# Attention and feed-forward on one core: the order of the first loads, the first k turned by blocks, and a split last tile

## The chip, the cores and the metric

The kernel runs on one core of one Trainium2 chip. The metric is the device time of one execution in microseconds (us); lower is better. The median of 6 runs before the change is 440.61 us (439.31 to 441.51).

## What is computed

Grouped-query attention, followed by a feed-forward layer with a squared relu. There are 8 batches, 16 query heads on 4 key/value heads (four query heads share one), 384 positions and 64 elements a head. The feed-forward takes the 3072 rows of attention output (8 x 384) through 1024 -> 2048 -> 1024.

```python
k = np.repeat(k, 4, axis=1); v = np.repeat(v, 4, axis=1)
scores = q @ k.transpose(0, 1, 3, 2) / sqrt(64)
attn = exp(scores - max(scores)); attn = attn / (sum(attn) + 1e-9)
x = (attn @ v).transpose(0, 2, 1, 3).reshape(3072, 1024)
out = maximum(x @ w_in, 0) ** 2 @ w_out
```

Inputs and output are float32; the kernel computes in bfloat16 with float32 accumulation.

## The kernel before

**A recorder.** The program is written as one list of operations (`R.add`, line 23). Each names its engine, what it reads and what it writes. From that list the recorder derives semaphores: an operation waits for the last writer of what it reads, and for writer and readers of what it overwrites; `after` adds further waits. Each engine runs its own operations in the order of the list, so a wait holds up all that stands behind it on that engine. DMAs are issued by an engine too: SP ("sync"), ACT ("scalar") or GpSimd ("gpsimd", POOL in the profile); an issue that waits holds up that engine's queue.

**Units.** The batches are called b0 to b7 here. A batch has 8 pairs of query heads (`NPB`), so there are 64 pairs; pair n of b0 uses k group n // 2. The 384 positions are three blocks of 128 (`NJ`). For a pair, scores are made transposed (keys on the partitions), exponentiated on ACT into `expT`, and multiplied with `v_aug` (v with a column of ones, so that the sum comes along) on PE into the bank `po`; DVE divides (`rinv`, `o_sb`, lines 416 and 419). Output tiles are transposed into `xT`, which the feed-forward reads: up-projection (line 437), relu on DVE (444), square on ACT (446), down-projection (455), copy to `y_sb` on DVE (464), store by SP (467).

**b0, the start.** b0's operands come as float32 by plain loads: k group 0 and then v and k groups 1 to 3 from SP (`first_k`, line 201; v, line 214), q in four pieces from ACT (`first_q`, line 207). Group 0 of k is cast and duplicated on DVE (`dup_k`, line 235), as is the first q piece (`cast_q`, line 230). All the others are cast on GpSimd. They are transposed on PE by a matmul against an identity and copied out of PSUM by DVE (`turn_on_pe`, lines 302 and 310; `first_kT`, `first_qT`). In the loop `for n in range(NPB)` the scores come block by block (`scores_unit`, 362 and 368), the turns of the next pair between them, and `attend(n - 1, ...)` in two halves. `idle(...)` are matmuls of zeros, with no use but to keep PE busy.

**GpSimd's order at the start** (lines 240 to 266): cast_q(1), cast of v, dup_k(1), load_q(1), cast_q(2), load_k(1), cast_q(3), load_w_in(0), cast_q(4), dup_k(2), load_w_in(1), and so on to cast_q(7), load_v(1), the remaining weight blocks, load_w_out(0 and 1), and then k, q and v of b2. The loads of this list convert float32 to bfloat16 on the way; they go through one software queue, in this order. `load_q(1)` is b1's q, 768 KB as bfloat16; `load_k(1)` is b1's k, 192 KB.

**b1 and later.** b1's k is duplicated by DVE in `dup_all_k(1)` (line 326), at the end of n = 3 in the list, and turned on PE between the pairs 4 to 7 of b0 and after them. From b2 on `prepare(b)` (line 330) duplicates k on DVE and lets SP issue transposing DMAs: one for k (line 333, it reads `k_dup`), two for q (line 340, they read `q_st`, where `load_q(b)` puts it). Each finished pair of b1 and later goes to `xT` by a transposing DMA on SP (`put_x`, line 424). SP's list around b1 is: put_x and stores of b0's output, `prepare(2)`, then again put_x of the pairs 12 to 15 and stores in turn.

**The feed-forward.** It is a generator of small steps; `fill` takes as many of them between the attention parts as a credit allows. Batch b's feed-forward starts when attention of batch b + 1 is under way. An up step for one chunk of 128 hidden columns takes the eight `xT` tiles in two groups of four. A down tile (128 rows x 512 columns) accumulates 16 matmuls in one of two banks `f_ps` (`down_step`, line 450). At the end only down tiles of b7 are left; the last one is followed by its copy and its store.

Of the kernel before, what the change touches and what calls it, by code (L numbers as in the profile page):

```python
# [106 lines left out]
def bass_gqa_attention__then__ffn_squared_relu_kernel(  # L107
# [11 lines left out]
    B, H, S, D = 8, 16, 384, 64  # L119
    HKV = 4  # L120
    NJ = S // 128
# [6 lines left out]
    NST, NKS, NEX, NXT, NHR, NY, NO = 3, 2, 3, 3, 3, 4, 4  # L128

    R = Recorder(nc)  # L130
# [7 lines left out]
    k_f = sb("k_f", [128, HKV, NJ, D], f32)  # L138
# [58 lines left out]
            moe_w_out[:, i * 512:(i + 1) * 512].rearrange("(c p) f -> p c f", p=128)),  # L197
            writes=[("w_out", i)], dma=f"wo{i}")

    def first_k(g0, g1):  # L200
        R.add("sync", lambda e: e.dma_start(
            k_f[:, g0:g1].rearrange("p g j d -> p g (j d)"),
            k[0, g0:g1].rearrange("g (p j) d -> p g (j d)", j=NJ)),
            writes=[("k_f", g) for g in range(g0, g1)], dma=f"kf{g0}")

    def first_q(c0, c1):
        R.add("scalar", lambda e: e.dma_start(
            q_f[:, 2 * c0:2 * c1, :], q[0, 2 * c0:2 * c1].rearrange("h (p j) d -> p h (j d)", j=NJ)),
            writes=[("q_f", c) for c in range(c0, c1)], dma=f"qf{c0}")

    first_k(0, 1)
    first_q(0, 1)
    first_q(1, 2)
    R.add("sync", lambda e: e.dma_start(
        v_f.ap().rearrange("p g j d -> p g (j d)"), v[0].rearrange("g (p j) d -> p g (j d)", j=NJ)),
        writes=["v_f"], dma="vf")
    first_q(2, 4)
    first_k(1, 4)
    first_q(4, 8)

    R.add("vector", lambda e: e.memset(warm[:], 0.0), writes=["warm"])  # L221
    R.add("gpsimd", lambda g: g.memset(ident[:], 0.0), writes=["ident"])
# [6 lines left out]
    def cast_q(c, eng="gpsimd"):  # L229
        R.add(eng, lambda g: g.tensor_copy(q_st[0][:, 2 * c:2 * c + 2, :], q_f[:, 2 * c:2 * c + 2, :]),  # L230
              reads=[("q_f", c)], writes=[("q_st", 0, c)])

    def dup_k(g, eng):
        src = k_f[:, g].unsqueeze(2).to_broadcast([128, NJ, 2, D])
        R.add(eng, lambda e: e.tensor_copy(k_dup[0][:, g * NJ:(g + 1) * NJ], src),
              reads=[("k_f", g)], writes=[("k_dup", 0, g)])

    dup_k(0, "vector")
    cast_q(0, "vector")
    cast_q(1)  # L240
    R.add("gpsimd", lambda g: g.tensor_copy(
        v_aug[0][:, :, 0:D], v_f.ap().rearrange("p g j d -> p (g j) d")),
        reads=["v_f"], writes=[("v_aug", 0)])
    dup_k(1, "gpsimd")
    load_q(1)
    cast_q(2)
    load_k(1)
    cast_q(3)
    load_w_in(0)
    cast_q(4)  # L250
# [43 lines left out]
            return f_ps[i - 5].ap().bitcast(bf16)[:, 0:S], ("f_ps", i - 5)  # L294
        return sc_bf[:, i, 0:S], ("sc", i)

    def turn_on_pe(src, src_keys, dst, dst_key, banks, eng="vector"):
        ps, key = turn_bank(banks)

        def tr(pe):  # L300
            for t in range(NJ):
                m = pe.matmul(ps[:, t * 128:(t + 1) * 128], src[:, t * 128:(t + 1) * 128], ident[:],  # L302
                              is_transpose=True)
            return m

        R.add("tensor", tr, reads=[*src_keys, "ident"], writes=[key])
        if eng == "scalar":
            R.add(eng, lambda e: e.copy(dst, ps), reads=[key], writes=[dst_key])
        else:
            R.add(eng, lambda e: e.tensor_copy(dst, ps), reads=[key], writes=[dst_key])  # L310

    def first_kT(g, b=0, banks=RING):
        turn_on_pe(k_dup[b][:, g * NJ:(g + 1) * NJ].rearrange("p a x d -> p (a x d)"), [("k_dup", b, g)],
                   kT[b][:, g], ("kT", b, g), banks)

    def first_qT(c, b=0, banks=RING):
        turn_on_pe(q_st[b][:, 2 * c:2 * c + 2, :].rearrange("p h e -> p (h e)"), [("q_st", b, c)],
                   qT[b][:, c], ("qT", b, c), banks)

    def first_oT(c, banks=RING, eng="vector"):  # L320
        turn_on_pe(o_sb[c % NO].ap().rearrange("p i s d -> p (i s d)"), [("o_sb", c % NO, x) for x in range(2)],
                   xT[0][:, c], ("xT", 0, c), banks, eng)

    def dup_all_k(b, eng="vector"):
        src = k_st[b % NKS].ap().rearrange("p g j d -> p (g j) d").unsqueeze(2)
        R.add(eng, lambda e: e.tensor_copy(  # L326
            k_dup[b % 2][:, :, :, :], src.to_broadcast([128, HKV * NJ, 2, D])),
            reads=[("k_st", b % NKS)], writes=[("k_dup", b % 2, g) for g in range(HKV)])

    def prepare(b):  # L330
        st = b % NST
        dup_all_k(b)
        R.add("sync", lambda e: e.dma_start_transpose(
            kT[b % 2].ap().rearrange("p g (j c) -> p (g j) c", j=NJ),
            k_dup[b % 2].ap().rearrange("p a x d -> p (a x d)")),
            reads=[("k_dup", b % 2, g) for g in range(HKV)],
            writes=[("kT", b % 2, g) for g in range(HKV)], dma=f"kt{b % 2}")
        for part in range(2):
            cs = range(4 * part, 4 * part + 4)
            R.add("sync", lambda e, cs=cs: e.dma_start_transpose(  # L340
                qT[b % 2][:, cs.start:cs.stop, :].rearrange("p h (t c) -> p (h t) c", t=NJ),
                q_st[st][:, 2 * cs.start:2 * cs.stop, :].rearrange("p h e -> p (h e)")),
                reads=[("q_st", st, c) for c in cs], writes=[("qT", b % 2, c) for c in cs],
                dma=f"qt{b % 2}_{part}")
# [5 lines left out]

    def operands(p):
        b, c = p // NPB, p % NPB
        return kT[b % 2][:, c // 2], qT[b % 2][:, c], [("kT", b % 2, c // 2), ("qT", b % 2, c)]

    def scores_unit(p, j):
        u = (p * NJ + j) % 2
        kt, qt, keys = operands(p)

        def sc(pe):
            for x in range(2):  # L360
                rows = slice(64 * x, 64 * x + 64)
                m = pe.matmul(sc_ps[:, 2 * u + x, 0:S], kt[rows, j * 128:(j + 1) * 128], qt[rows, :])  # L362
            return m

        R.add("tensor", sc, reads=keys, writes=[("sc", 2 * u), ("sc", 2 * u + 1)])
        src = sc_ps[:, 2 * u:2 * u + 2, 0:S].rearrange("p x (t c) -> p x t c", t=NJ)
        dst = expT[p % NEX][:, j, :].rearrange("p (t x c) -> p x t c", x=2, t=NJ)
        R.add("scalar", lambda e: e.activation(dst, src, AF.Exp, scale=0.125),  # L368
              reads=[("sc", 2 * u), ("sc", 2 * u + 1)], writes=[("expT", p % NEX, j)])

    def scores_pair(p):
        kt, qt, keys = operands(p)
        half = NJ * S

        def piece(pe, x, j, c0, c1):
# [54 lines left out]
    tiles = [0]  # L430
# [16 lines left out]
                  reads=[("hr", r)], writes=[("h2T", b % 2, c)])  # L447
        return (k1 - k0) * 165

    def down_step(b, i, jj, part, u):  # L450
        yb = (b * 2 * NJ + jj * NJ + i) % NY

        def mm(pe):
            for c in range(4 * part, 4 * part + 4):
                m = pe.matmul(f_ps[u][:, :], h2T[b % 2][:, c, i * 128:(i + 1) * 128],  # L455
                              w_out_sb[:, c, jj * 512:(jj + 1) * 512],
                              start=(c == 0), stop=(c == NFC - 1))
            return m

        R.add("tensor", mm, reads=[("w_out", jj)] +  # L460
              [("h2T", b % 2, c) for c in range(4 * part, 4 * part + 4)], writes=[("f_ps", u)])
        if part == 3:
            half = slice(jj * 512, (jj + 1) * 512)
            R.add("vector", lambda e: e.tensor_copy(y_sb[yb][:, :], f_ps[u][:, :]),  # L464
                  reads=[("f_ps", u)], writes=[("y", yb)])
            rows = out[b * S:(b + 1) * S, :].rearrange("(p j) f -> j p f", j=NJ)[i]
            R.add("sync", lambda e: e.dma_start(rows[:, half], y_sb[yb][:, :]),
                  reads=[("y", yb)], writes=[("out", b, i, jj)], dma=f"y{yb}")
        return 4 * 216

    def feed_forward(b):
        first = 0
        if b == 0:
            for c, k in [(c, k) for c in range(3) for k in (0, 2, 4)] + [(c, 6) for c in range(3)]:
                yield up_step(b, c, k, k + 2, c, c)
            first = 3
        for c in range(first, NFC):
            for k in range(0, NKC, 4):
                yield up_step(b, c, k, k + 4, tiles[0] % 2, tiles[0] % NHR)
            tiles[0] += 1  # L480
        for jj in range(2):
            for i in range(NJ):
                for part in range(4):
                    yield down_step(b, i, jj, part, tiles[0] % 2)
                tiles[0] += 1


    ready = [0]
# [21 lines left out]
    turns += [lambda banks=RING, c=c: first_qT(c, 1, banks) for c in range(NPB)]  # L510

    idle(13)
    first_kT(0, banks=(4,))
    idle(1)
    first_qT(0, banks=(6,))
    for n in range(NPB):
        ring = (4, 6) if n < 4 else RING
        scores_unit(n, 0)
        if n >= 4:
            turns.pop(0)()  # L520
        else:
            idle(2 if n == 0 else 1)
        if n >= 1:
            attend(n - 1, 0)
        scores_unit(n, 1)
# [48 lines left out]
        ready[0] = max(0, n // NPB - 1)  # L574
    while next(ffn, None):
        pass
    R.add("sync", lambda e: e.nop(), reads=[("out", b, i, jj) for b in range(B) for i in range(NJ) for jj in range(2)])
    R.emit()


# [26 lines left out]
```

The softmax here doesn't subtract the row's maximum and nothing guards it: scores larger than these inputs give would overflow.

## Time and profile before

| what | us |
|---|---|
| median of 6 runs | 440.61 (439.31 to 441.51) |
| the profiled execution, its time | 439.11 |
| its span from the first to the last instruction | 436.9 |
| PE busy in the span | 427.5 (98%) |
| ACT, DVE, GpSimd busy | 199.4, 164.7, 34.2 |

All numbers of the profile come from that one execution. A row of instructions has a start, a length, the engine, the line, the operation, output tile <- input tiles and how many. "SPq", "ACTq" and "POOLq" are the instructions by which an engine issues DMAs. A part in brackets tells the idle time before an instruction and who ended it. A row of a DMA issue has the size of one and the time from issue to landing.

The first 40 us as a table of who does what first:

| event | starts at, us |
|---|---|
| first k (group 0) duplicated on DVE, first q piece cast | 3.40, 3.95 |
| first scores, first exp | 5.50, 6.04 |
| cast_q(1), cast of v, dup_k(1) on GpSimd | 5.72, 6.16, 7.17 |
| load_q(1), cast_q(2), load_k(1), cast_q(3), load_w_in(0) on GpSimd | 7.63, 8.91, 9.36, 10.11, 10.55 |
| dup_all_k(1) on DVE | 17.00 |
| last exp of b0 ends | 28.51 |
| first up-projection of the feed-forward | 27.90 |

ACT's 24 exps of b0 take 0.81 each; ACT is idle 5.8 us before them in sum, 1.66 of it before the exp at 19.46.

At the end of the span the last down tile's matmuls run to 433.76, the copy from 433.78 to 434.47, the last store is issued at 434.50 and takes 2.0 from issue to landing.

### The profile page before, as it was taken

Reading aid. Unit: us, or ns where it says so; the run is one execution under the profiler, and the core shown is the slowest. Engines: PE = TensorE matmul, PEld = TensorE weight load, DVE = VectorE, ACT = ScalarE, POOL = GpSimd, SP = SyncE. Lnnn points to the kernel's source line nnn. Section 1 sums busy time; section 2 is a strip of 40 time slices with the busy share of each in tenths; the row PEclk is TensorE's granted clock in tenths of the full one; section 3 lists DMA queues with packets and bytes.
Section 4 is the critical chain, followed back from the end, with each engine's and each line's share of the span. In section 5 each row is a group of like instructions: output and inputs, shape, how many; then the busy total and the mean of one; then the engine's idle time right before and its main releaser. Section 6 shows DMA issues by size and latency. Waiting matters only on the chain.

```text
span 436.9 us, 8195 instructions
## 1 busy us (share of the span) xinstructions
PE 427.5 (98%) x3580; PEld 239.2 (55%) x3615; DVE 164.7 (38%) x354; ACT 199.4 (46%) x210; POOL 34.2 (8%) x50
## 2 busy tenths in 40 slices
PE   8899999999999999999999999999999999999997
PEld 4565655556545654466545665556654565546543
DVE  2665433244323442244423443334522443324311
ACT  4766743466334563256523654336643366103300
POOL 5930000020000100020000200011000000000000
PEclk9999999999999999999999999999999999999999
DMA  7999999366722945238621856229542200220011
GB/s 223 192 197 203 193 206 195 125 79 68 167 66 68 121 86 105 89 61 102 128 92 59 111 76 135 69 81 127 70 109 75 67 11 18 68 83 24 2 72 72
DMA packets 95939, 44.70 MB, mean 102 GB/s; under 512 B 74400, under 2 KB 89760, under 8 KB 95904
## 3 DMA queue, kind: packets, MB, share of 16 engines
q0 software_dynamic: 34288, 16.65, 30.6%
q1 hardware_dynamic: 59504, 25.96, 25.4%
q10 hardware_dynamic: 2112, 1.57, 1.1%
q8 instruction: 28, 0.46, 0.4%
q14 instruction: 7, 0.06, 0.0%
HBM read 35.65 MB, written 12.58 MB: 110 GB/s over the span
## 4 chain that ended last, share of the span: by engine, by line
PE 93%; DMA 4%; DVE 2%; issue 1%; POOL 1%; SPq 0%
PE f_ps L437 38%; PE f_ps L455 37%; PE po L406 8%; PE sc_ps L378 7%; DMA k_st<-in_k_dram 2%; DMA k_f<-in_k_dram 1%; PE sc_ps L362 1%; DMA xT<-o_sb 1%; PE sc_ps L302 0%; PE f_ps L302 0%; DVE o_sb L419 0%; DVE y_sb L464 0%; POOL q_st L181 0%; PE sc_ps L437 0%; DVE k_dup L326 0%
## 5 line engine op out<-in xcount | busy, mean ns | idle before, releaser
L437 PE MATMUL f_ps<-xT,w_in_sb 128*128 128x384 bf16 x1016 | 181.3, 326 | 0.2
L455 PE MATMUL f_ps<-w_out_sb,h2T 128*128 128x512 bf16 x733 | 175.0, 379 | 2.3 <-issue 0.6
L395 ACT ACTIVATE expT<-sc_ps 128x2304 bf16<-128x2304 f32 x56 | 116.8, 2086 | 100.8 <-PE sc_ps L378 99.1
L437 PEld LDWEIGHTS f_ps<-xT,w_in_sb 128*128 128x128 bf16 x1016 | 92.5, 98 | 61.3 <-issue 6.4
L446 ACT ACTIVATE h2T<-hr 128x384 bf16<-128x384 f32 x128 | 66.6, 521 | 104.3 <-DVE hr L444 102.8
L455 PEld LDWEIGHTS f_ps<-w_out_sb,h2T 128*128 128x128 bf16 x768 | 69.2, 98 | 76.3 <-issue 5.5
L444 DVE TENSOR_SCALAR hr<-f_ps 128x384 f32<-128x384 f32 x127 | 70.6, 556 | 99.9 <-PE f_ps L437 99.9
L464 DVE COPY y_sb<-f_ps 128x512 f32<-128x512 f32 x48 | 33.2, 691 | 107.5 <-PE f_ps L455 107.1
L406 PEld LDWEIGHTS po<-v_aug,expT 128*128 128x128 bf16 x1143 | 52.1, 98 | 22.5 <-ACT expT L368 0.9
L406 PE MATMUL po<-v_aug,expT 128*128 128x65 bf16 x1143 | 56.9, 194 | 0.9 <-DVE o_sb L419 0.4
L378 PE MATMUL sc_ps<-qT,kT 64*128 64x128 bf16 (+2 forms) x504 | 37.2, 271 | 0.2
L419 DVE TENSOR_TENSOR o_sb<-po,rinv 128x384 bf16<-128x384 f32 x64 | 35.5, 554 | 2.2
L378 PEld LDWEIGHTS sc_ps<-qT,kT 64*128 64x128 bf16 x504 | 20.6, 94 | 21.7 <-issue 16.1
L416 DVE RECIPROCAL rinv<-po 128x6 f32<-128x6 f32 x64 | 12.3, 192 | 43.6 <-PE po L406 43.6
L167 POOL DMA_DIRECT2D k_st<-in_k_dram x7 | 5.3, 758 | 256.9 <-DMA xT<-o_sb 256.9
L368 ACT ACTIVATE expT<-sc_ps 128x768 bf16<-128x768 f32 x24 | 18.7, 810 | 5.8 <-PE sc_ps L362 5.1
L362 PE MATMUL sc_ps<-qT,kT 64*128 64x384 bf16 x48 | 8.9, 367 | 0.5 <-DVE qT L310 0.5
L181 POOL DMA_DIRECT2D q_st<-in_q_dram x7 | 8.3, 1190 | 0.0
L272 PE MATMUL f_ps<-warm 128*128 128x256 bf16 x23 | 6.2, 386 | 1.0 <-DVE warm L221 1.0
L189 POOL DMA_DIRECT2D w_in_sb<-in_moe_w_in_dram x8 | 7.0, 890 | 0.0
L174 POOL DMA_DIRECT2D v_st<-in_v_dram x7 | 5.5, 779 | 0.0
L326 DVE COPY k_dup<-k_st 128x1536 bf16<-128x1536 bf16 x7 | 4.2, 597 | 2.6 <-DMA k_st<-in_k_dram 2.6
(44 smaller groups left out, 53.6 us busy)
## 6 DMA issues: line engine op xcount, KB each, us to landing
out_dram<-y_sb SPq DMA_DIRECT2D x48, 256.0 KB, 2.0
q_st<-in_q_dram POOLq DMA_DIRECT2D x7, 768.0 KB, 10.6
w_in_sb<-in_moe_w_in_dram POOLq DMA_DIRECT2D x8, 512.0 KB, 13.1
w_out_sb<-in_moe_w_out_dram POOLq DMA_DIRECT2D x2, 2048.0 KB, 34.2
k_st<-in_k_dram POOLq DMA_DIRECT2D x7, 192.0 KB, 3.6
v_st<-in_v_dram POOLq DMA_DIRECT2D x7, 192.0 KB, 11.0
xT<-o_sb SPq DMA_TRANSPOSE x56, 2.3
q_f<-in_q_dram ACTq DMA_DIRECT2D x1, 768.0 KB, 7.8
```

Source lines behind the costliest of these rows:

```text
L362: m = pe.matmul(sc_ps[:, 2 * u + x, 0:S], kt[rows, j * 128:(j + 1) * 128], qt[rows, :])
L368: R.add("scalar", lambda e: e.activation(dst, src, AF.Exp, scale=0.125), reads=[("sc", 2 * u), ("sc", 2 * u + 1)], writes=[("expT", p % NE ...
L378: return pe.matmul(sc_flat[:, at + c0:at + c1], kt[rows, j * 128:(j + 1) * 128], qt[rows, c0:c1])
L395: R.add("scalar", lambda e: e.activation(dst, src, AF.Exp, scale=0.125), reads=sc_keys, writes=[("expT", p % NEX, j) for j in range(NJ)])
L406: m = pe.matmul(acc[:, i, s, :], expT[p % NEX][:, j, f * 128:(f + 1) * 128], v_aug[b % 2][:, g * NJ + j, :], start=(j == 0), stop=(j == NJ ...
L416: R.add("vector", lambda e: e.reciprocal(rinv_v, acc[:, :, ss, D:D + 1]), reads=[acc_key], writes=[("rinv", p % 2)])
L419: R.add("vector", lambda e: e.tensor_tensor(o_sb[p % NO][:, :, ss, :], acc[:, :, ss, 0:D], rb, ALU.mult), reads=[acc_key, ("rinv", p % 2)] ...
L437: m = pe.matmul(acc[:, 0:S], w_in_sb[:, kc, c * 128:(c + 1) * 128], xT[b % NXT][:, kc, :], start=(kc == 0), stop=(kc == NKC - 1))
L444: R.add("vector", lambda e: e.tensor_scalar_max(hr[r][:, :], acc[:, 0:S], 0.0), reads=[key], writes=[("hr", r)])
L446: R.add("scalar", lambda e: e.activation(h2T[b % 2][:, c, :], hr[r][:, :], AF.Square), reads=[("hr", r)], writes=[("h2T", b % 2, c)])
L455: m = pe.matmul(f_ps[u][:, :], h2T[b % 2][:, c, i * 128:(i + 1) * 128], w_out_sb[:, c, jj * 512:(jj + 1) * 512], start=(c == 0), stop=(c = ...
L464: R.add("vector", lambda e: e.tensor_copy(y_sb[yb][:, :], f_ps[u][:, :]), reads=[("f_ps", u)], writes=[("y", yb)])
```

## The change

Four things change.

First, the order of b0's loads. ACT's queue issues its four q pieces as before. On SP, v is now issued only after the first q piece has landed (`after=[landed]`), and k groups 1 to 3 behind it in the same queue.

Second, on GpSimd, `load_k(1)` stands right behind `dup_k(1)`, and `load_q(1)` behind `cast_q(2)`; that is, b1's k is issued ahead of b1's q.

Third, k group 0 of b0 is duplicated, turned and copied in two parts: block 0 alone ahead of the first scores, blocks 1 and 2 behind the first `scores_unit`. The key of a `kT` or `k_dup` tile has the block in it now, so that scores of block j wait for block j alone.

Fourth, the last down tile of b7 (128 x 512) is made as 384 columns and then 128 columns, each with its 16 matmuls, its copy and its store.

```diff
     first_k(0, 1)
-    first_q(0, 1)
+    landed = first_q(0, 1)
     first_q(1, 2)
+    first_q(2, 4)
+    first_q(4, 8)
     R.add("sync", lambda e: e.dma_start(
         v_f.ap().rearrange("p g j d -> p g (j d)"), v[0].rearrange("g (p j) d -> p g (j d)", j=NJ)),
-        writes=["v_f"], dma="vf")
-    first_q(2, 4)
+        writes=["v_f"], dma="vf", after=[landed])
     first_k(1, 4)
-    first_q(4, 8)
...
-    def dup_k(g, eng):
-        src = k_f[:, g].unsqueeze(2).to_broadcast([128, NJ, 2, D])
-        R.add(eng, lambda e: e.tensor_copy(k_dup[0][:, g * NJ:(g + 1) * NJ], src),
-              reads=[("k_f", g)], writes=[("k_dup", 0, g)])
-
-    dup_k(0, "vector")
+    def dup_k(g, eng, j0=0, j1=NJ):
+        src = k_f[:, g, j0:j1].unsqueeze(2).to_broadcast([128, j1 - j0, 2, D])
+        R.add(eng, lambda e: e.tensor_copy(k_dup[0][:, g * NJ + j0:g * NJ + j1], src),
+              reads=[("k_f", g)], writes=[("k_dup", 0, g, j) for j in range(j0, j1)])
+
+    dup_k(0, "vector", 0, 1)
     cast_q(0, "vector")
+    dup_k(0, "vector", 1, NJ)
     cast_q(1)
...
     dup_k(1, "gpsimd")
+    load_k(1)
+    cast_q(2)
     load_q(1)
-    cast_q(2)
-    load_k(1)
     cast_q(3)
...
     def scores_unit(p, j):
         u = (p * NJ + j) % 2
-        kt, qt, keys = operands(p)
+        kt, qt, keys, k_keys = operands(p)
+        keys = keys + k_keys[j:j + 1]
...
-    def down_step(b, i, jj, part, u):
+    def down_step(b, i, jj, part, u, c0=0, c1=512):
...
-                m = pe.matmul(f_ps[u][:, :], h2T[b % 2][:, c, i * 128:(i + 1) * 128],
-                              w_out_sb[:, c, jj * 512:(jj + 1) * 512],
+                m = pe.matmul(f_ps[u][:, 0:c1 - c0], h2T[b % 2][:, c, i * 128:(i + 1) * 128],
+                              w_out_sb[:, c, jj * 512 + c0:jj * 512 + c1],
...
-                for part in range(4):
-                    yield down_step(b, i, jj, part, tiles[0] % 2)
-                tiles[0] += 1
+                last = (b, i, jj) == (B - 1, NJ - 1, 1)
+                for c0, c1 in ((0, 384), (384, 512)) if last else ((0, 512),):
+                    for part in range(4):
+                        yield down_step(b, i, jj, part, tiles[0] % 2, c0, c1)
+                    tiles[0] += 1
...
     idle(13)
-    first_kT(0, banks=(4,))
+    first_kT(0, banks=(4,), j1=1)
     idle(1)
     first_qT(0, banks=(6,))
     for n in range(NPB):
...
         if n >= 4:
             turns.pop(0)()
+        elif n == 0:
+            first_kT(0, banks=(4,), j0=1)
+            idle(2)
         else:
-            idle(2 if n == 0 else 1)
+            idle(1)
```

`first_kT` and `turn_on_pe` take the range of blocks j0 to j1 and turn and copy only these.

More of the change, by code (lines that the diff above doesn't have):

```diff
@@ L198, in load_w_out, with first_k @@
             writes=[("w_out", i)], dma=f"wo{i}")
-    def first_k(g0, g1):
+    def first_k(g0, g1, after=()):
         R.add("sync", lambda e: e.dma_start(
@@ L203, in first_k @@
             k[0, g0:g1].rearrange("g (p j) d -> p g (j d)", j=NJ)),
-            writes=[("k_f", g) for g in range(g0, g1)], dma=f"kf{g0}")
+            writes=[("k_f", g) for g in range(g0, g1)], dma=f"kf{g0}", after=after)
     def first_q(c0, c1):
-        R.add("scalar", lambda e: e.dma_start(
+        return R.add("scalar", lambda e: e.dma_start(
             q_f[:, 2 * c0:2 * c1, :], q[0, 2 * c0:2 * c1].rearrange("h (p j) d -> p h (j d)", j=NJ)),
@@ L295, in turn_bank, with turn_on_pe @@
         return sc_bf[:, i, 0:S], ("sc", i)
-    def turn_on_pe(src, src_keys, dst, dst_key, banks, eng="vector"):
+    def turn_on_pe(src, src_keys, dst, dst_keys, banks, eng="vector", n=NJ):
         ps, key = turn_bank(banks)
         def tr(pe):
-            for t in range(NJ):
+            for t in range(n):
                 m = pe.matmul(ps[:, t * 128:(t + 1) * 128], src[:, t * 128:(t + 1) * 128], ident[:],
@@ L307, in turn_on_pe, with first_kT @@
         if eng == "scalar":
-            R.add(eng, lambda e: e.copy(dst, ps), reads=[key], writes=[dst_key])
+            R.add(eng, lambda e: e.copy(dst, ps[:, 0:n * 128]), reads=[key], writes=dst_keys)
         else:
[L310 to L314, printed above, removed]
+            R.add(eng, lambda e: e.tensor_copy(dst, ps[:, 0:n * 128]), reads=[key], writes=dst_keys)
+    def first_kT(g, b=0, banks=RING, j0=0, j1=NJ):
+        turn_on_pe(k_dup[b][:, g * NJ + j0:g * NJ + j1].rearrange("p a x d -> p (a x d)"),
+                   [("k_dup", b, g, j) for j in range(j0, j1)], kT[b][:, g, j0 * 128:j1 * 128],
+                   [("kT", b, g, j) for j in range(j0, j1)], banks, n=j1 - j0)
     def first_qT(c, b=0, banks=RING):
         turn_on_pe(q_st[b][:, 2 * c:2 * c + 2, :].rearrange("p h e -> p (h e)"), [("q_st", b, c)],
-                   qT[b][:, c], ("qT", b, c), banks)
+                   qT[b][:, c], [("qT", b, c)], banks)
     def first_oT(c, banks=RING, eng="vector"):
         turn_on_pe(o_sb[c % NO].ap().rearrange("p i s d -> p (i s d)"), [("o_sb", c % NO, x) for x in range(2)],
-                   xT[0][:, c], ("xT", 0, c), banks, eng)
+                   xT[0][:, c], [("xT", 0, c)], banks, eng)
     def dup_all_k(b, eng="vector"):
@@ L327, in dup_all_k @@
             k_dup[b % 2][:, :, :, :], src.to_broadcast([128, HKV * NJ, 2, D])),
-            reads=[("k_st", b % NKS)], writes=[("k_dup", b % 2, g) for g in range(HKV)])
+            reads=[("k_st", b % NKS)], writes=[("k_dup", b % 2, g, j) for g in range(HKV) for j in range(NJ)])
     def prepare(b):
@@ L335, in prepare @@
             k_dup[b % 2].ap().rearrange("p a x d -> p (a x d)")),
-            reads=[("k_dup", b % 2, g) for g in range(HKV)],
-            writes=[("kT", b % 2, g) for g in range(HKV)], dma=f"kt{b % 2}")
+            reads=[("k_dup", b % 2, g, j) for g in range(HKV) for j in range(NJ)],
+            writes=[("kT", b % 2, g, j) for g in range(HKV) for j in range(NJ)], dma=f"kt{b % 2}")
         for part in range(2):
@@ L352, in operands @@
         b, c = p // NPB, p % NPB
-        return kT[b % 2][:, c // 2], qT[b % 2][:, c], [("kT", b % 2, c // 2), ("qT", b % 2, c)]
+        return kT[b % 2][:, c // 2], qT[b % 2][:, c], [("qT", b % 2, c)], [("kT", b % 2, c // 2, j) for j in range(NJ)]
     def scores_unit(p, j):
         u = (p * NJ + j) % 2
-        kt, qt, keys = operands(p)
+        kt, qt, keys, k_keys = operands(p)
+        keys = keys + k_keys[j:j + 1]
         def sc(pe):
@@ L371, in scores_pair @@
     def scores_pair(p):
-        kt, qt, keys = operands(p)
+        kt, qt, keys, k_keys = operands(p)
+        keys = keys + k_keys
         half = NJ * S
@@ L462, in down_step @@
         if part == 3:
-            half = slice(jj * 512, (jj + 1) * 512)
-            R.add("vector", lambda e: e.tensor_copy(y_sb[yb][:, :], f_ps[u][:, :]),
-                  reads=[("f_ps", u)], writes=[("y", yb)])
+            R.add("vector", lambda e: e.tensor_copy(y_sb[yb][:, c0:c1], f_ps[u][:, 0:c1 - c0]),
+                  reads=[("f_ps", u)], writes=[("y", yb, c0)])
             rows = out[b * S:(b + 1) * S, :].rearrange("(p j) f -> j p f", j=NJ)[i]
-            R.add("sync", lambda e: e.dma_start(rows[:, half], y_sb[yb][:, :]),
-                  reads=[("y", yb)], writes=[("out", b, i, jj)], dma=f"y{yb}")
-        return 4 * 216
+            R.add("sync", lambda e: e.dma_start(rows[:, jj * 512 + c0:jj * 512 + c1], y_sb[yb][:, c0:c1]),
+                  reads=[("y", yb, c0)], writes=[("out", b, i, jj, c0)], dma=f"y{yb}_{c0}")
+        return 4 * 216 * (c1 - c0) // 512
     def feed_forward(b):
@@ L576, in bass_gqa_attention__then__ffn_squared_relu_kernel @@
         pass
-    R.add("sync", lambda e: e.nop(), reads=[("out", b, i, jj) for b in range(B) for i in range(NJ) for jj in range(2)])
+    R.add("sync", lambda e: e.nop(), reads=[("out", b, i, jj, c) for b in range(B) for i in range(NJ) for jj in range(2) for c in (0, 384)])
     R.emit()
```

## The prediction

> **What bounds the kernel now.** I read the page first: PE is busy 98% of 436.9 us, and "PE 93%" heads the chain that ended last, so only stretches where PE waits can be won or lost. Two lie in the change's reach. The first is in the chain, cut to the first 40 us (start, length, what):
>
> ```profile
> 1.66 5.46 DMA k_f<-in_k_dram
> ...
> 7.17 0.51 POOL k_dup L235
> 7.68 1.24 POOL q_st L181
> 8.92 0.44 POOL q_st L230
> 9.36 7.62 DMA k_st<-in_k_dram
> 16.98 0.02 issue
> 17.00 0.87 DVE k_dup L326
> ```
>
> GpSimd sits on the chain: k groups 1 to 3 of b0 land at 7.12, then GpSimd duplicates group 1, issues b1's q (1.24), casts a q chunk, and only then issues b1's k, which comes in behind q at 16.98. DVE had been idle 0.81 us by then (its own row, "[0.81 <-DMA k_st<-in_k_dram]"), and PE 1.0 us behind it. That is what the change aims at.
>
> The second is the chain between 79 and 90 us. It is the only later place in the chain where a transfer stands:
>
> ```profile
> 81.19 0.57 DVE o_sb L419
> 81.76 0.02 issue
> 81.77 2.28 DMA xT<-o_sb
> 84.05 0.05 issue
> 84.10 1.47 PE f_ps L437 x8
> ```
>
> b1's first up-projection needs the last x tile of b1, and that transpose is issued by SP. SP's own row of instructions from 60 to 90 us shows how free SP is (start, length):
>
> ```profile
> 63.78 2.53 SPq L333 DMA_TRANSPOSE kT<-k_dup  x1
> 70.46 3.15 SPq L340 DMA_TRANSPOSE qT<-q_st  x2
> 73.65 1.01 SPq L467 DMA_DIRECT2D out_dram<-y_sb  x1
> 74.71 1.20 SPq L424 DMA_TRANSPOSE xT<-o_sb  x1
> 75.96 1.90 SPq L467 DMA_DIRECT2D out_dram<-y_sb  x1
> 77.90 1.21 SPq L424 DMA_TRANSPOSE xT<-o_sb  x1
> 79.15 0.58 SPq L467 DMA_DIRECT2D out_dram<-y_sb  x1
> 79.78 1.20 SPq L424 DMA_TRANSPOSE xT<-o_sb  x1
> 81.02 0.58 SPq L467 DMA_DIRECT2D out_dram<-y_sb  x1
> 81.77 1.18 SPq L424 DMA_TRANSPOSE xT<-o_sb  x1
> ```
>
> From 70.46 SP works without a pause until 81.60, and the decisive put_x is issued at 81.77, 0.02 after DVE's o_sb ends (81.75). SP has caught up by only some 0.15 us. What started it at 70.46 is in SP's waits:
>
> ```profile
> SPq L340 <- DMA q_st<-in_q_dram: 4.1, 1, 4.1
> ```
>
> So SP stood 4.1 us until b2's q landed (issued at 23.97, 46.5 us to landing: 70.47). That load is second to last of the prologue's queue on GpSimd. From 11 us on that queue never runs dry: DMA share 1.24 or more and 165 to 206 GB/s in every window I took up to 70. Whatever shifts the queue's beginning shifts 70.46, and from there 84.10, one for one beyond 0.15 us. How it begins, in windows (last two columns DMA share and GB/s):
>
> ```profile
> 4.00:9.50 5.50, 5.04 (x34) 2.32 (x33) 1.38 (x4) 3.29 (x5) 3.60 (x6) 1.00 1.03 323
> 9.50:10.00 0.50, 0.50 (x5) 0.22 (x4) 0.00 (x0) 0.10 (x1) 0.50 (x1) 1.00 0.43 27
> 10.00:10.50 0.50, 0.50 (x8) 0.50 (x7) 0.17 (x1) 0.50 (x1) 0.50 (x2) 1.00 0.57 38
> 10.50:11.00 0.50, 0.50 (x13) 0.36 (x10) 0.50 (x3) 0.21 (x1) 0.50 (x2) 1.00 1.17 122
> ```
>
> b0's first loads fill the DMA engines to 9.5, and GpSimd's queue takes over, slowly, from load_q(1) issued at 7.63.
>
> **Part 1, v and k groups 1 to 3 behind the first q.** Landings by the DMA issue rows: group 0 of k 0.74 + 2.6 = 3.3; first q 0.73 + 3.2 = 3.9; v 1.20 + 4.7 = 5.9; k1-3 at 7.12; last q 2.2 + 7.8 = 10.0. After, SP waits for the first q. It shares the engines with k alone, so I take 3.6 (bounds 3.3, when group 0 of k lands, and 3.9, as now). SP then issues v at 3.65 and k1-3 0.46 later (as now, 1.20 to 1.66). Nothing else waits behind them on SP before put_x at 46 us. All first loads hold 2.36 MB, the engines stay full with q, so the end near 9.5 stays and the two late loads share with the last q. First bytes come some 1.1 us after issue (first k: issued 0.74, 35 GB/s in the window 1.50 to 2.00). From 4.75, half of 340 GB/s carries v and k1-3 (0.69 MB) in 4.05 us: 8.8, landing some 0.45 later: **k1-3 at 9.3** (+2.2), v about 7.5. Bounds: 7.1, if they take all the bandwidth (0.69/0.34 = 2.0 us instead of 4.05), and 10.0, with the last q. The issue-to-landing row as it is gives 4.1 + 5.5 = 9.6.
>
> **Part 2, GpSimd's order.** v's cast (0.83) ends at 8.3, and attend(0, 0) wants it at 8.65, when the third exp ends: covered by 0.3 us, and if v were 0.5 later PE would lose 0.2. dup_k(1) 9.35 to 9.8; load_k(1) to 10.55 (row 0.76); cast_q(2) to 11.05; load_q(1) from 11.0 instead of 7.63; cast_q(3) ends 12.8 instead of 10.6. What waits for GpSimd: first_kT(1) on PE (9.79 now) just fits; first_qT(2) (10.08 now) waits until 11.05, **1.0 us**, with attend(0, 1), scores_unit(1, 2) and so the exps behind it. cast_q(3) to cast_q(7) and dup_k(2), dup_k(3), all some 2.2 later, still come before PE's turn (first_qT(3) 12.73 now, 13.7 then; first_kT(2) 15.19, 16.2 against 14.6).
> b1's k alone in the queue takes about 3.6 us (the page's median) to 7.6 (now): it lands between 13.4 and 17.4, I take 13.6, nearest the row of loads on an empty queue. dup_all_k(1) then waits only for DVE's turn, 16.19 now. So the 0.81 is won, the 1.0 is lost, and part 3 gives 0.1: b1's k_dup ends about 0.1 us later than now (bounds -0.9 without the PE wait, +0.8 with k1-3 at 10.0).
>
> **The queue's shift.** load_q(1) took 8.2 us now: 11.0 + 8.2 = 19.2 with k in before it. Now both are in at 16.98. Shift **+2.2 us**. If b1's k has opened the queue, the slow opening (the three windows 9.5 to 11.0 carry 94 of 292 KB that 195 GB/s would) is saved: -1.0. With k1-3 from 7.1 to 10.0 the shift lies between -1.0 and +2.9; I take 2.2, the row of the same transfer. A page speaks against it: the Trainium skill, "DMA: Bandwidth & Descriptors", "Anatomy of one DMA - SWDGE (gpsimd) path", gives a software-issued load about 2.0 us plus bytes over 436 GB/s. By it b1's q (1.57 MB read) takes 5.6 us where this trace has 8.2, an estimate by which the queue would not shift and PE would lose nothing at 84; the trace's own row decides.
> Others that the shift reaches are covered: w_in block 0 lands at 19.8 (used 27.9), block 7 at 39.4 (used about 52), w_out at 49.5 (55.64) and 62.0 (69), v of b1 28.7 (33.96), k of b2 63.2, which holds DVE 2 us longer, until 65.9, while the y copy behind it, due at 64.78, frees a bank that PE wants at 69. With 2.2 more, they all still fit. Only q of b2 doesn't: SP would start at 72.66, reach put_x at 83.8, and PE restart at 86.15: **+2.05**, in which the start's 0.1 disappears.
>
> **Part 3, first k by blocks.** DVE's 0.55 becomes about 0.25 and 0.4, PE turns one block, not three (0.2 less), and copies a third; the other two turns and a second copy come behind the first scores, where idle matmuls stood. Gain at the first scores 0.4, at the second about 0.1, because PE's 0.4 of turns stands between.
>
> **Part 4, the last tile.** The y copy of 512 columns takes 0.69; relu of 384 takes 0.556, so 1.05 ns a column and 0.29 for 128: -0.40. The last store carries 64 KB instead of 256: its bytes take 0.75 of its 2.0 us (windows 435.25 to 436.0), a third of that now: -0.5. PE: 16 x (162 + 56) ns instead of 16 x 216, by the chain's 0.65 for four, 0.17 for three: +0.05. The first 384 columns (copy, issue 0.33) lie under the last 16 matmuls. **-0.85** (bounds -0.95, and -0.35 if the store gains nothing).
>
> The new keys change which block a wait names and add no instruction later on. **Sum:** +2.05 - 0.85 = **+1.2 us**. The profiled execution took 439.11 us around its span of 436.9, so 440.3 like for like; the median 440.61 stands 1.5 above it, and the forecast is 441.8.
>
> **Rivals.** (a) *SP absorbs it.* Two stores on SP took 1.01 and 1.90, where quiet ones take 0.33. If they shrink when the queue has drained, SP wins back up to 2.25 and reaches put_x in time: +0.1 - 0.85, about 439.8. Against it: they follow the q transposes, which move too. (b) *Faster:* SP's late loads outrun the last q, k1-3 land near 7.1 and the queue comes 0.9 earlier; the start gains 0.9 and 84 lets it through: -0.9 - 0.85, 438.9. It decides from k1-3 at 7.6 or earlier; for it: SP carried 0.79 MB by 7.1 of some 1.6 in all, though not more than half. (c) *Slower through the start alone:* k1-3 at 10.0 gives PE a wait of 1.7 at 10 us, where a pair of 128x384 matmuls still takes 0.50 and from 10.8 on 0.34. If PE stays slow for a few us more, the start would lose over 2.05 and decide: about 442.8. "TensorE: Matmul & The Clock Gate", Part 1, says the clock rises after about 3.4 us of activity in a free-running window; no row here shows what a wait does to it.
>
> **Chances.** A measurement of this kernel can't tell less than 0.3% (1.3 us) from no change. Forecast 0.62, from 440.6 (shift 1.2) to 442.8 (2.9): 0.37 of it above 441.9, 0.25 below; (a) 0.16; (b) 0.14; (c) 0.08. So slower 0.45, same 0.41, faster 0.14. The range 439.0 to 443.2 leaves out part of (b) and the top of (c); the forecast's own is 440.6 to 442.8.
>
> **What would show it.** Right: load_q(1) issued near 11.0; b1's k landed before DVE's turn, with no wait at L326; SP's q wait ending near 72.6; the xT transfer on the chain until 86. Wrong: k1-3 landed before 8; no wait of PE near 84 longer than now; a last store as long as before.

## The result and the profile after

The changed kernel takes **443.62 us** (median of 20 runs, 442.75 to 444.27) against 441.13 for the kernel before (46 runs, 438.54 to 442.79): ratio 1.0060, 95% interval 1.0048 to 1.0072, 2.5 us slower. The forecast was 441.8, slower by 1.2; the measured time lies above its range. The profiled execution took 443.22 us around a span of 441.0, so the two profiles are 4.1 us apart and the two medians 2.5: the profile of before, 439.11, lies 2.0 below the median of its kernel, that of after only 0.4 below its own.

The beginning of the chain of waits after (start, length, what):

```profile
0.73 3.16 DMA q_f<-in_q_dram
3.89 0.02 issue
3.90 6.56 DMA v_f<-in_v_dram
10.46 0.05 issue
10.52 0.83 POOL v_aug L242
11.35 0.46 POOL k_dup L235
11.80 0.82 POOL k_st L167
12.63 0.53 POOL q_st L230
13.15 0.05 issue
13.20 0.50 PE f_ps L303 x3
```

The chain no longer runs through k groups 1 to 3, but through v: issued at 3.90, once the first q is in, it takes 6.56 us where it took 4.7, and lands at 10.46. k groups 1 to 3, issued at 4.35, land 6.9 later, at 11.25. From v's cast on, all of GpSimd's list comes late: load_q(1) is issued at 13.07 instead of 7.63. PE waits for v_aug, as its list of waits says:

```profile
PE po L410 <- POOL v_aug L242: 3.3, 1, 3.3
...
PE f_ps L441 <- DMA xT<-o_sb: 0.7, 1, 0.7
```

The second of these is the wait near 84, in which PE needs b1's last x tile. SP's rows there, after:

```profile
75.22 3.87 SPq L342 DMA_TRANSPOSE qT<-q_st  x2
...
84.85 1.20 SPq L428 DMA_TRANSPOSE xT<-o_sb  x1
86.09 0.57 SPq L470 DMA_DIRECT2D out_dram<-y_sb  x1
86.71 1.21 SPq L428 DMA_TRANSPOSE xT<-o_sb  x1
```

and the chain behind them:

```profile
86.71 2.30 DMA xT<-o_sb
89.01 0.05 issue
89.06 1.47 PE f_ps L441 x8
```

b2's q lands at 75.22 instead of 70.46, SP works without a pause from there to 86.66, and PE restarts at 89.06 instead of 84.10: 4.96 later.

SP is not the only one that is late there. PE reaches its first up-projection at 32.27 instead of 27.90, 4.4 late before b2's q plays any part, and DVE has the last x tile of b1 ready at 86.14 instead of 81.75, as late as that:

```profile
32.27 1.15 PE f_ps L441 x6
85.58 0.56 DVE L423 TENSOR_TENSOR o_sb<-po,rinv 128x384 bf16<-128x384 f32 x1
```

So SP ends the wait, but only some 0.5 us behind PE and DVE. The late v reaches 84 by two paths of nearly the same length: through the software queue and SP, and through PE's own loss at the start.

The last tile, on the other hand, gives back what it should. DVE's last rows (start, length):

```profile
437.88 0.56 DVE L467 COPY y_sb<-f_ps 128x384 f32<-128x384 f32 x1 [1.91 <-PE f_ps L459]
438.78 0.29 DVE L467 COPY y_sb<-f_ps 128x128 f32<-128x128 f32 x1 [0.34 <-PE f_ps L459]
```

The last copy takes 0.29 instead of 0.69, and from its end (439.07) to the end of the span (441.0) there are 1.93 us where there were 2.42 (434.47 to 436.9): together -0.9. 4.96 less 0.9 is the 4.1 between the profiles.

The DMA queues show where v was (packets, MB, share of the 16 engines); q10 is ACT's queue, q1 SP's. Before, with SP's loads issued early, from 3 to 6 us:

```profile
q1 hardware_dynamic: 877, 0.66, 67.7%
q10 hardware_dynamic: 507, 0.37, 37.5%
```

After, from 4.75 to 6.75:

```profile
q10 hardware_dynamic: 839, 0.63, 101.5%
```

and from 7.5 to 8.75:

```profile
q1 hardware_dynamic: 353, 0.27, 65.4%
q10 hardware_dynamic: 226, 0.16, 39.5%
```

SP had issued v at 3.90, and from 4.75 to 6.75 not one packet of it moves: the engines are full of q pieces that ACT had queued by 2.8. SP's queue gets its share only as these run out.

### The profile page after: what moved, and what is told of

Its sections match the earlier page's. It is cut to its first block, busy times and chain, and to the rows that moved or that the text cites. A ratio compares the mean times of both kernels' runs of the same rounds, so it can differ in the third digit from the quotient of the medians.

```text
span 441.0 us, 8227 instructions
## 1 busy us (share of the span) xinstructions
PE 428.8 (97%) x3596; PEld 240.7 (55%) x3631; DVE 164.6 (37%) x357; ACT 199.4 (45%) x210; POOL 34.2 (8%) x50
## 4 chain that ended last, share of the span: by engine, by line
PE 94%; DMA 3%; DVE 2%; issue 1%; POOL 1%
PE f_ps L441 38%; PE f_ps L459 37%; PE po L410 8%; PE sc_ps L382 7%; DMA v_f<-in_v_dram 1%; PE sc_ps L365 1%; DMA q_f<-in_q_dram 1%; PE sc_ps L303 1%; DMA xT<-o_sb 1%; PE f_ps L303 1%; DVE o_sb L423 0%; PE f_ps L273 0%; DVE qT L311 0%; DVE y_sb L467 0%; PE sc_ps L441 0%
## 5 line engine op out<-in xcount | busy, mean ns | idle before, releaser
L459 PE MATMUL f_ps<-w_out_sb,h2T 128*128 128x512 bf16 (+2 forms) x749 | 175.0, 375 | 2.3 <-issue 0.6
L459 PEld LDWEIGHTS f_ps<-w_out_sb,h2T 128*128 128x128 bf16 x784 | 70.2, 98 | 75.7 <-issue 5.5
L467 DVE COPY y_sb<-f_ps 128x512 f32<-128x512 f32 (+2 forms) x49 | 33.3, 680 | 105.9 <-PE f_ps L459 105.5
L273 PEld LDWEIGHTS f_ps<-warm 128*128 128x128 bf16 x23 | 2.8, 126 | 4.1 <-DVE warm L221 1.0
```

The lines of the kernel that those rows point to most:

```text
L459: m = pe.matmul(f_ps[u][:, 0:c1 - c0], h2T[b % 2][:, c, i * 128:(i + 1) * 128], w_out_sb[:, c, jj * 512 + c0:jj * 512 + c1], start=(c == 0 ...
L467: R.add("vector", lambda e: e.tensor_copy(y_sb[yb][:, c0:c1], f_ps[u][:, 0:c1 - c0]), reads=[("f_ps", u)], writes=[("y", yb, c0)])
```

## The experiments

Runs that were measured together are called a job here; each job has its own runs of the kernel before. Theory A was: v and the k groups come behind the whole q, and GpSimd's fixed order hands their lateness to the software queue and so to PE at 84. Its rivals: the swap of b1's k and q costs most (C), the late transfers have a fixed start-up (B), PE's half clock after its wait costs most (D), SP catches up at 84 anyway (E).

**e1, the load order put back.** The kernel after with this edit:

```diff
-    landed = first_q(0, 1)
+    first_q(0, 1)
     first_q(1, 2)
-    first_q(2, 4)
-    first_q(4, 8)
     ...
-        writes=["v_f"], dma="vf", after=[landed])
+        writes=["v_f"], dma="vf")
+    first_q(2, 4)
     first_k(1, 4)
+    first_q(4, 8)
```

> The kernel after with only the order of b0's loads put back: v and k groups 1 to 3 issued at once on SP. Theory A (late v and k groups arrive behind the whole q, GpSimd's fixed order carries their lateness into the software queue and to PE): v lands near 5.9 again, load_k(1) is issued near 7.7, no wait of PE for v_aug, b2's q lands within 0.5 of 70.5, and with the shorter tail (-0.85) the time is 0.5 to 1.5 us below the kernel before. Theory C (b1's k ahead of its q opens the software queue twice and costs most of the loss): 1 to 3 us above the kernel before.

Measured: 439.18 us against 440.72 before (ratio 0.9966, 0.9947 to 0.9986), so 1.5 below. v's cast starts at 6.16, load_k(1) is issued at 7.57, PE has no wait for v_aug; b2's q lands at 71.30, 0.8 later than in the profile of before, a little over the 0.5 expected. By the medians the other three parts together are a gain, and the load order turns the change into a loss. (Profile against profile e1 gains nothing: its span is 437.3 against 436.9.)

**e2, only the load order changed.** The kernel before with the same lines the other way round.

> The kernel before with only v and k groups 1 to 3 queued on SP behind the first q. Theory A: v lands at 10 to 10.5, PE waits over 3 us for v_aug, PE restarts at 84 some 4 to 5 us later than in the profile of before; about 3.5 us above the kernel before by medians (the loss of the change, 2.5, and the tail's gain, 0.85, which this one lacks). Theory C: within 0.5 us of the kernel before.

Measured: 444.41 (6 runs) against 440.72 (1.0083, 1.0054 to 1.0112): +3.7. PE's waits, the chain at 84, and SP's row ahead of the decisive put_x, which leaves at 88.38:

```profile
PE po L406 <- POOL v_aug L241: 3.6, 1, 3.6
PE f_ps L302 <- DVE k_dup L326: 1.4, 1, 1.4
```

```profile
87.79 0.57 DVE o_sb L419
88.36 0.02 issue
88.38 2.29 DMA xT<-o_sb
90.67 0.04 issue
90.72 1.31 PE f_ps L437 x7
```

```profile
85.98 0.33 SPq L467 DMA_DIRECT2D out_dram<-y_sb  x1
```

The size is that of theory A: the late loads alone cost more than the whole change. C falls as the main cause, as b1's k is still behind its q here. The path is another one in this profile: SP is free from 86.31 and put_x leaves right behind DVE's o_sb, so here PE's own lateness decides (its first down-projection starts at 62.03 instead of 55.64), not SP. This execution took 445.69, 1.3 above the median of its six runs, and PE restarts 6.6 late, not the 4 to 5 expected.

**e3, only the swap.** The kernel before with load_k(1) ahead of cast_q(2) and load_q(1).

> The kernel before with only b1's k issued ahead of b1's q on GpSimd. Theory A: k_dup of b1 no longer waits for the load (0.8 gained at 17 us), but b2's q stays at 70 to 71 and SP's stretch to the last put_x of b1 lets through 0.2 at most: between -0.3 and +0.3 us. Theory C: b2's q lands over 1 us later and the time is 1 to 2 us above the kernel before.

Measured: 439.50 against 440.72 (0.9973, 0.9956 to 0.9991): a gain of 1.2, where I had expected none. In its profile b1's k_dup starts at 15.26 with no wait for the load (17.00 before), and b2's q lands at 71.07, 0.6 later than before. Near 84 PE waits:

```profile
PE f_ps L437 <- DMA xT<-o_sb: 1.0, 1, 1.0
```

So what the swap wins at the start is given back at 84, as expected, and its profile (437.6) is no shorter than that of before (436.9). The gain in the medians must have another source; e4 points to one.

**e4, only the split tile.**

> The kernel before with only the last down tile split into 384 and 128 columns. By the working: last copy 0.69 to 0.29 (-0.40), last store's bytes a quarter (-0.5), PE +0.05: -0.85 us. Rival (a small store is not faster than a large one, only the copy counts): -0.35 us.

Measured: 440.80 against 440.72 (0.9989, 0.9969 to 1.0010): inconclusive by the times, whose interval holds -0.85 as well as nothing. In the profile, copy and end are as in the kernel after: 2.0 us from the end of the last copy (436.90) to the end of the span, 438.9. But this execution is 2 us longer than the profile of before, though nothing differs ahead of the tail. Its windows (the third number from the end is the granted TensorE clock, 1.00 being full speed), and below them two of the same windows before:

```profile
16.00:18.00 2.00, 0.57 (x6) 0.22 (x4) 0.23 (x1) 1.47 (x2) 2.00 (x4) 1.00 1.48 194
18.00:20.00 2.00, 1.33 (x14) 0.86 (x14) 1.52 (x5) 0.00 (x0) 2.00 (x3) 0.60 1.45 197
20.00:25.00 5.00, 5.00 (x49) 3.45 (x48) 2.50 (x8) 3.22 (x4) 5.00 (x6) 0.50 1.45 197
25.00:27.00 2.00, 1.91 (x29) 1.18 (x26) 1.70 (x6) 1.33 (x3) 1.40 (x2) 0.95 1.47 197
```

```profile
18.00:20.00 2.00, 1.56 (x28) 1.14 (x28) 1.35 (x4) 0.54 (x1) 2.00 (x3) 1.00 1.45 197
20.00:25.00 5.00, 4.91 (x74) 3.19 (x73) 3.64 (x13) 4.57 (x7) 5.00 (x6) 1.00 1.45 197
```

In e4 PE waits 1.8 us for b1's k_dup near 17, and from 18.4 to 25 it is granted half its clock. PE is then late by itself, as the chain near 84 shows:

```profile
83.97 0.57 DVE o_sb L419
84.53 0.02 issue
84.55 2.29 DMA xT<-o_sb
86.84 0.05 issue
86.89 1.47 PE f_ps L437 x8
```

put_x leaves right behind DVE's o_sb, with no queue in front of it: PE decides here, not SP. Over the 64 runs of the kernel before in the first two jobs the time follows the mean granted clock of the run: 438.87 at 1.000 (median of 7), 440.72 at 0.996 (31), 441.78 at 0.992 (26). The profile of before on which the prediction stands was one with the clock at 1.000, among the shortest of its kernel. And 9 of the 12 runs of e3 and 11 of the 12 of e1 are at 0.999 or more, against 7 of the 64 of before: without PE's wait for b1's k the clock mostly stays up. That is the likeliest source of the swap's gain in the medians; no run tests it by itself.

**e5, the last q piece behind v.** The kernel after, with:

```diff
-    first_q(4, 8)
     ...
     first_k(1, 4)
+    R.add("sync", lambda e: e.dma_start(
+        q_f[:, 8:16, :], q[0, 8:16].rearrange("h (p j) d -> p h (j d)", j=NJ)),
+        writes=[("q_f", c) for c in range(4, 8)], dma="qf4")
```

> The kernel after with the last q piece (heads 8 to 15, 768 KB as float32) issued on SP behind v and k groups 1 to 3, instead of on ACT ahead of them. If SP's late transfers come behind whatever ACT had queued by then (theory A), v now has only q pieces 1 to 3 ahead of it: v lands between 6 and 7.5 instead of 10.5, k groups 1 to 3 by 8.5, load_k(1) is issued below 9.5 and the time falls to 439.5 to 441. If the lateness comes from the wait and a fixed start-up of late transfers (theory B), v still lands past 9 and the time stays above 443.

Measured: 442.02 against 441.30 before (1.0016, 1.0005 to 1.0027), so 1.6 below the kernel after of another job, but not the 439.5 to 441 expected. v lands at 8.2, between what theory A (6 to 7.5) and theory B (past 9) had expected. GpSimd's rows:

```profile
8.23 0.83 POOL L244 CAST v_aug<-v_f 128x768 bf16<-128x768 f32 x1 [3.37 <-DMA v_f<-in_v_dram]
9.86 0.51 POOL L237 CAST k_dup<-k_f 128x384 bf16<-128x384 f32 x1 [0.80 <-DMA k_f<-in_k_dram]
10.31 0.88 POOL L167 DMA_DIRECT2D k_st<-in_k_dram  x1
```

v, issued at 3.81, now takes 4.4 us from issue to landing, about the 4.7 of before. The rows of its issue before and in e5 (KB, us to landing):

```profile
v_f<-in_v_dram SPq DMA_DIRECT2D x1, 384.0 KB, 4.7
v_f<-in_v_dram SPq DMA_DIRECT2D x1, 384.0 KB, 4.4
```

Half of its lateness goes with the q piece ahead of it; the other half, the 2.6 by which it is issued later, stays. So both the wait itself and the place in the line cost.

**e6 and e10, PE kept busy through its wait.** The kernel after, with zeros multiplied while v is on its way:

```diff
+        if n == 1:
+            idle(30)
         if n >= 1:
             attend(n - 1, 0)
```

> The kernel after with 30 idle matmuls (3.2 us at full clock) ahead of the attend that waits for v, so that PE is busy through the wait. Theory A (the software queue's lateness decides at 84, PE's speed before that doesn't): the granted clock no longer falls to half between 9 and 19 us, and the time stays within 0.5 us of the kernel after, 443.6. Theory D (the half clock between 9 and 19 us makes the loss): 1.5 to 2.5 us below the kernel after, 441 to 442.

Measured: 442.72 (1.0027, 1.0012 to 1.0042 to the before of its job), 0.9 below the after of another job. That is between the two expectations. The same edit was measured again as e10, in one job with the kernel after, e9:

> The kernel after once more, on the same chip and in the same job as the next one, since the first run with PE kept busy came out 0.9 us below the after measured in another job. As measured there: 2 to 3 us above the kernel before, PE at half clock from about 9 to 19 us.

> The kernel after with 30 idle matmuls ahead of the attend that waits for v, beside the kernel after itself. Theory A (the queue alone): within 0.3 us of e9. Theory D (the half clock after PE's wait is a part of the loss): 0.7 to 1.5 us below e9.

Measured: e9 443.50, e10 442.95 (5 runs each; 1.0069, 1.0048 to 1.0091, and 1.0056, 1.0036 to 1.0075). 0.55 below, between the bounds of A and of D. The intervals against before overlap, but four of e10's five runs lie below all five of e9. In both profiles of the kept-busy kernel a pair of 128x384 matmuls takes 0.34 between 12 and 19; in e9 it takes 0.50 up to 16, in the kernel after up to 18. PE's speed is restored and little comes of it, since b2's q lands just as late (75.28 in e6, 74.86 in e10, 75.08 in e9). PE reaches its first down-projection 0.8 earlier in e10 than in e9 (59.10, 59.91), then waits 0.7 ahead of the scores at 80.37, just behind SP's q transposes (issued until 80.00), and restarts after 84 only 0.25 earlier (88.65, 88.90). D falls as the main cause; a part of about half a microsecond is likely. The zeros fill the wait for v and do not shorten it, so these runs say nothing on what the wait itself would cost without the late queue.

**e7, a longer queue.** e1 with one more weight block ahead of b2's k and q:

```diff
+    R.add("gpsimd", lambda g: g.dma_start(
+        h2T[1][:, 0:NKC, 0:WC], moe_w_in[:, 0:WC].rearrange("(c p) f -> p c f", p=128)),
+        writes=[("h2T", 1, c) for c in range(NKC)], dma="spare")
     load_k(2)
```

> The kernel with the load order put back (e1), and one more weight block (512 KB as bfloat16, 2.6 us at 197 GB/s) loaded into a buffer that is overwritten later, ahead of b2's k and q in the software queue. Theory A: b2's q lands 2.6 us later and PE restarts at 84 by as much later: 2.3 to 2.7 us above e1, 441.5 to 442. Theory E (SP catches up, the queue's end does not decide): within 0.5 us of e1, 439.2.

Measured: 442.10 (1.0024, 1.0006 to 1.0042) where e1 has 0.9966: 0.58%, or 2.6 us, the size that A gives. E falls by the times, and the path through the queue and SP is shown to cost by itself, with v on time. The single profile shows less, in the same place: b2's q lands at 72.79 (71.30 in e1), PE restarts at 86.49 (85.28).

**e8, a way around 84.** e1 with load_k(2) and load_q(2) ahead of load_w_out(1).

> The kernel with the load order put back (e1), and b2's k and q loaded ahead of the second half of w_out. Theory A: b2's q lands near 57, SP has no backlog at 80, PE's wait for xT at 84 (0.8 in e1) goes to 0.3 or less: 0.5 to 1.0 us below e1, 438.2 to 438.7. If w_out's second half, 5 us later at 67, comes too late for the down tiles at 69, a new wait of PE there: at or above e1.

Measured: 440.53 (0.9993, 0.9972 to 1.0013), above e1 (0.9966), though the two intervals overlap: the alternative named. The second half of w_out comes too late,

```profile
PE f_ps L459 <- DMA w_out_sb<-in_moe_w_out_dram: 2.3, 1, 2.3
```

and SP has no backlog near 84, to no use: PE is late by itself.

**e11, only the blocks.** The kernel before with only the first k turned block by block.

> The kernel before with only the first k duplicated, turned and copied block by block. By the working: the first scores 0.4 earlier, the second 0.1, and the wait for b1's k at 17 us takes it back: within 0.3 us of the kernel before. Rival (an earlier first exp shortens b0): 0.4 us below.

Measured: 441.02 against 441.09 (1.0007, 0.9990 to 1.0024): no change that can be told, as expected. The first scores start at 5.16 (5.50 before), and the wait for b1's k at 17 takes it back: 1.7 us in this profile.

**e12, a faster order.** e1 with b1's k issued ahead of v's cast, and b1's q right behind dup_k(1):

```diff
     cast_q(1)
+    load_k(1)
     ...
     dup_k(1, "gpsimd")
-    load_k(1)
-    cast_q(2)
     load_q(1)
+    cast_q(2)
```

> The kernel with the load order put back (e1), and b1's k issued ahead of v's cast, b1's q right behind dup_k(1). The software queue starts some 1.4 us earlier for k and 0.7 for q, into the gap between 9.5 and 11. Theory A: b2's q lands 0.5 to 1 us earlier and the time is 0.3 to 0.8 below e1, near 438.5. Rival (k's packets only take the place of q's in the first loads, or v's cast comes late for PE): the same as e1 or above.

Measured: **438.45** against 441.09 (0.9956, 0.9939 to 0.9972), 2.6 below the kernel before and 5 below the changed one: faster than both. It is also below e1's 0.9966, though the two intervals overlap. In its profile b2's q lands at 71.11, only 0.2 earlier than in e1, not the 0.5 to 1 expected; PE still waits at 84:

```profile
PE f_ps L441 <- DMA xT<-o_sb: 1.5, 1, 1.5
```

So the queue's end is what remains to be won there. Why it came out below e1 is not settled: a part may be the clock (1.0 in all 9 runs), a part b2's q in the other runs.

## Why the prediction was right in direction and wrong in size

**The mechanism held for the queue.** SP's unbroken stretch from b2's q to the last put_x of b1, with the start of the software queue behind it, ends the wait at 84 in the kernel after; e7 lengthens the queue alone by 2.6 us and loses 2.6 by the medians (1.2 in its profile, where b2's q came 1.5 later). The way in which the sum gets the queue's shift held too: load_q(1), issued at 13.07, takes 8.7 (8.2 before) and lands at 21.8, 4.8 behind the 16.98 at which both of b1's loads were in before. b1's k did land before DVE's turn (k_dup at 20.82, with no wait at the load), so the 0.81 at 17 us was won. What the mechanism left out is the start: PE's own loss there, 0.1 in the sum, was 4.4.

**The step that failed** is in part 1: "From 4.75, half of 340 GB/s carries v and k1-3 (0.69 MB) in 4.05 us: 8.8". SP's two loads got no half; in the two microseconds from 4.75 they got none at all. v landed at 10.46 instead of about 7.5, k groups 1 to 3 at 11.25 instead of 9.3, beyond even the bound of 10.0, which took for granted that they come in with the last q, not after it (the last q landed at 9.3). The row of before (4.7 and 5.5 from issue to landing) had been set aside for that bandwidth sum, though it pointed the right way; but it, too, was a row in which SP's loads had been queued alongside ACT's. The runs measure it: without the last q piece ahead, v takes 4.4 (e5); with it, 6.6 and, in e9, 7.1. The Trainium skill, "DMA: Bandwidth & Descriptors", "Queues, rings and completion order", says that a DMA engine goes round the queues it has work for, packet by packet. By that SP would have had its half from about 5 on; the 839 packets to none say otherwise here. Whether the engines served ACT's queue out first, or SP's descriptors were not yet made, the traces don't tell.

**What followed from it.** (1) "covered by 0.3 us": the cover over attend(0, 0) was gone, and PE waited 3.3. With that, and with half the clock from about 9 to 19, it came to its first up-projection 4.4 late; the sum's 0.1 for the start, which was to disappear behind the queue, is mis-sized by as much. (2) load_q(1) at 13.07 instead of 11.0. (3) The queue's shift: 4.76 instead of 2.2; GpSimd itself was 4.1 late from load_w_in(0) on (14.66 for 10.55). (4) PE's restart: +4.96 instead of +2.05. Of this, 4.4 would have come through PE and DVE alone; SP adds the rest.

**Part 2's own cost**, the wait of PE at first_qT(2), 1.0 by the sum, is 0.2 in the profile after, since PE now comes there later itself. In the kernel after, load_q(1) takes its 8.7 with only b1's k ahead of it in the queue, which is again slow to start: 101 GB/s in the window 14 to 16 against 195 later. The formula of the Trainium skill's page in the prediction (5.6 us for b1's q, and so no shift) does not fit that either.

**Part 3**: first scores at 5.28 and second at 6.33 instead of 5.50 and 6.47, so 0.2 and 0.1 for 0.4 and 0.1. The first q landed at 3.89, as before, where 3.6 had been taken: k was not all that it shared the engines with, since ACT's queue moved 0.40 MB by then, twice the piece itself. **Part 4**: -0.85 by the working, about -0.9 in the profiles of after (e4's is a little less, -0.8).

**The base.** A single profile stood for the kernel before, and it was among the shortest of its executions. Carried to the median by adding 1.5, the forecast took for granted that the change shifts all runs alike. It doesn't: before, the time goes with the mean clock of the run, 2.9 us from 1.000 to 0.992, while after it hardly does (443.72 at 0.988, 443.46 at 1.000). That the late queue evens this out is argued, not shown, and the record of the clock is not safe there: e9's profile has 1.000 with matmuls at half speed up to 16 us. With every term sized right, like for like, the sum is +4.1; by the medians it is +2.5.

Rival (a), that SP absorbs it, fell: of the two slow stores one shrank (1.90 to 0.58), but SP's q transposes took 3.87 instead of 3.15, and one put_x 2.09 instead of 1.21. Rival (b) would have needed k groups at 7.6. Rival (c) saw the start's loss: PE's wait was 3.3 where it had 1.7, with half the clock behind it, and its path to 84 was only some 0.5 us shorter than SP's. What (c) did not see is that the queue would move with it.

## What to carry to other kernels

The transfer that was held back here to give another one room lost twice: by the wait, and by its place behind what another queue had issued meanwhile. Before delaying a load, look at who consumes it in a fixed order: here a cast on an engine that also issues the next 10 MB of loads. And follow every path on which the lateness travels: here two of nearly the same length met at 84. Take the base of a sum from several executions where the run times spread.

## What was not expected of the hardware

Without v and k groups 1 to 3 beside it, the first q piece (192 KB) still took 3.16 us from issue to landing (3.2 before, with them). It did not have the engines to itself: up to 3.9 us ACT's queue moved 0.40 MB, so about as much of the later q pieces had gone with it, and 0.10 MB of k.

A wait of PE of 1.8 us at 17 us went with half the clock from 18.4 to 25 (e4), one of 3.3 us from 8.2 on with half the clock from about 9 to 19 (after); in the profile of before a wait of 1.0 us at 17 went with none. The times of the kernel before spread over 4 us with it. The clock column itself has to be checked against the matmuls: in e9 it reads 1.00 from 9 us on, yet a pair of 128x384 matmuls takes 0.50 up to 16 us and 0.34 from 16.6 on.
